# Seven small experts: taken in the order of their token counts, with fixed capacities and one loop at the end

## Chip, core and metric

The kernel runs on one core of a Trainium2 chip. The metric is the device time of one execution in microseconds, as the median of the runs shown. TensorE (PE) multiplies matrices, VectorE (DVE), ScalarE (ACT) and GpSimd (POOL) work on elements, SyncE (SP) issues most of the transfers, and POOL issues the transfers whose rows are picked by a list (gathers and scatters).

## What is computed

An attention over blocks gives x (2304 tokens, 512 wide). A dense two-layer network follows, and then a layer of eight experts, of which each token uses one, or none. Only this last layer is touched:

```python
do_compute = (x @ w_skip) > 0
xc = x[do_compute]
e_idx = np.argmax(xc @ w_gate, axis=1)
for e in range(8):
    mask = e_idx == e
    h = np.maximum(xc[mask] @ w1[e], 0.0)       # w1[e]: 512 x 1024
    y[mask] = gate_w[mask, None] * (h @ w2[e])  # w2[e]: 1024 x 512
out[do_compute] = xc + y
```

How many tokens an expert gets is known only while the kernel runs.

## The kernel before

Attention and the dense network fill the first 660 us of the profiled execution. While the dense network ends, the router writes for each token one row (place, output row, gate) into a list in DRAM, ordered by expert (`lists_d`, three copies that are summed after loading). `base` holds how far each expert's part of the list is filled, so `base - eoff` is the count of each expert.

Expert 0 has tiles of 128 tokens that are computed with split numbers, in three products for each one (`expert_tile`, L948). The first two tiles always run; `more` (L1099) runs a further one behind a condition on the count, and a loop after the fourth.

Experts 1 to 7 are computed in fp32, in the order of their numbers. Their tokens stand in groups of 32 (`MG`), because TensorE can work on four blocks of 32 columns of the stationary operand side by side: a matmul of form 128\*32 uses a quarter of the array, one of form 128\*64 a half, one of 128\*128 the whole. `Groups` (L1166) has the first product of the first group in `first`, those of the further groups in `first_rest` (L1181, each behind a condition), the turning of the hidden values in `turn` (L1149; its second half behind the condition in L1188), the second product in `second` (L1158, conditions in L1193), and the sum of the four quarters, the scaling and the scatter in `end` (L1204, L1162, L1163). `spill` (L1221) has a block of 64 tokens behind a condition (L1224) and a loop behind another (L1226). Expert 7 stands behind a condition as a whole (L1245, L1250). Each such condition is a branch on all engines, on a count that each has in a register (L1071).

`load_expert` (L838) loads the 4 MB of one expert's weights into one of four places, in eight transfers on SP's queue (L851 for w1, L853 for w2). Experts 1 and 2 are loaded ahead of the lists, 3 and 4 behind `more`, each later one behind the expert whose place it takes. For every token list, `load_lists` and `find` (L629, L624) load and sum the copies and turn them to row numbers on DVE; `gather` (L634) fetches the token rows, `turn_x` (L903) turns them on PE.

The kernel's text is written as steps; a scheduler sets the order in which small instructions stand on each engine, unless they are pinned.

Of the kernel before, what the change touches and what calls it, by code (L numbers as in the profile page):

```python
# [10 lines left out]
F32 = mybir.dt.float32  # L11
F32R = mybir.dt.float32r
BF16 = mybir.dt.bfloat16
I32 = mybir.dt.int32
# [332 lines left out]
def attention_moe_kernel(  # L347
# [716 lines left out]
    cnti = RC.tile([128, E], I32, name="cnti")  # L1064
    nc.vector.tensor_tensor(out=cnti, in0=base, in1=eoff, op=ALU.subtract)


    lall = [lists(f"la{k_}", E) for k_ in range(KS)]
    llate = lists("lx", 1)
# [13 lines left out]
    xgs.insert(4, xgf[1])  # L1083
    xts = [[M3.tile([128, ND, 128], F32R, name=f"xt{i}{j}", bufs=1) for j in range(2)] for i in range(2)]
    xts = [xtf[0], xts[0], xtf[1], xts[1]]
    fourth = lane(lall[3], 0, xgs[0], xts[2])
    xws = [CV.tile([128, ND, 128], F32, name=nm, bufs=3) for nm in ("cv2", "cv2", "cv3")]
    firsts = [lane32(lall[0], e, xgs[e % 4], xws[e % 2]) for e in range(E)]
    for lx in (firsts[1], fourth, firsts[2], firsts[3]):
        gather(lx)  # L1090

    ahead1 = [lambda: turn_x(firsts[1])]

    def later(k_):
        if k_ == 3:
            return fourth
        return lane(lall[k_] if k_ < KS else llate, 0, xgs[4 + (k_ + 1) % 2], xts[2 + (k_ + 1) % 2])

    def more(k_, lx):  # L1099
        with nullcontext() if k_ == 1 else tc.If(nreg[0] > 128 * k_):  # L1100
            if k_ < KS:
                ahead = []
                nx = later(k_ + 1)
                if k_ + 1 < KS:
                    if nx is not fourth:
                        gather(nx)
                    ahead = [lambda: turn_x(nx)]
                finish = expert_tile(lx, ahead + (ahead1 if k_ == 1 else []))
                finish()
                more(k_ + 1, nx)  # L1110
            else:
                with tc.For_i(KS, (nreg[0] + 127) // 128, 1) as i:
                    load_lists(llate, lambda l: l[bass.ds(i * 128, 128), :].unsqueeze(1), nc.sync)
                    find(llate)
                    gather(lx)
                    turn_x(lx)
                    expert_tile(lx)()

    more(1, second)
    gather(firsts[4])  # L1120
    load_expert(3)
    load_expert(4)


    MG, MH = 32, 64
    pin = tc.keep_in_program_order
    h2 = [CV.tile([128, 512], F32, name=nm, bufs=3) for nm in ("cv2", "cv3")]
    hT, ev01, ev23 = (CV.tile([128, 2, 512], F32, name="raw", bufs=3) for _ in range(3))
    ev = [ev01[:, 0], ev01[:, 1], ev23[:, 0], ev23[:, 1]]
    hx = M3.tile([128, 512], F32, name="hs")  # L1130
    for t in (*h2, hT, ev01, ev23, hx, xws[2]):
        nc.gpsimd.memset(t, 0.0)
    sums = {m: M3.tile([128, m], F32, name=f"sum{m}", bufs=1) for m in (MG, MH)}
    for m, t in sums.items():
        nc.vector.reduce_sum(out=t, in_=ident.rearrange("p (s t) -> p t s", t=m), axis=AX.X)
    bank = lambda nm: ps3.tile([128, 512], F32, name=nm, tag="ps")

    def first_product(ph, e, x, m):

        s = 128 // m  # L1140
        w = F2 // s
        for c in range(ND):
            for j in range(s):
                pin(nc.tensor.matmul(ph[j * m : j * m + m], x[:, c], weights[e][0][c][:, j * w : j * w + w], start=(c == 0), stop=(c == ND - 1)))
# [152 lines left out]
```

## Time and profile before

| | us |
|---|---|
| median of 3 runs (837.49 to 839.02) | 838.4 |
| the profiled execution, its own time | 842.87 |
| its span, first to last instruction | 841.0 |

The span is what the trace covers; 1.87 us of the profiled execution lie around it. This execution is 4.5 us longer than the median, so a difference worked out on the trace is taken from the median. All times of rows are microseconds from the span's start.

### The profile page before, as it was taken

To read this page: it belongs to the slowest core of one execution; us is meant where nothing else is said; L and a number is where in the kernel's file an instruction comes from. 1 tells how busy PE (TensorE), PEld (TensorE's weight loads), DVE (VectorE), ACT (ScalarE), POOL (GpSimd) and SP (SyncE) were. 2 spreads that over 40 slices of the span, in tenths; PEclk is the share of its full clock that TensorE was granted. 3 is DMA by queue.
4 is the path that set the end of the run, shared out by engine and by line. 5 is a ranking of instruction groups with operands and counts; after the bars stand their busy time and mean duration, and the time that the engine had idled before them with its cause. 6 is when DMAs were issued, how large, how long until landed. Compare 5 with 4: busy or idle time off the path is not lost. (4 is left out here: it accounts for less than half of the span.)

```text
span 841.0 us, 13930 instructions
## 1 busy us (share of the span) xinstructions
PE 771.7 (92%) x4662; PEld 637.6 (76%) x4662; DVE 518.4 (62%) x1134; ACT 400.9 (48%) x921; POOL 355.6 (42%) x433
## 2 busy tenths in 40 slices
PE   6788989999999989999999999999999989988883
PEld 4567878888888978898999898888898767642430
DVE  6877789886987875675663599969213632111221
ACT  6787788786977975555452222222223412111110
POOL 2755446363454664454452432562424533100211
PEclk9889999999999999999999999999999999999999
DMA  6664474454433031752233564114014944294761
GB/s 165 155 164 130 117 174 109 105 156 124 111 96 85 16 115 46 244 181 100 74 87 116 153 182 154 39 43 162 22 76 151 342 78 92 95 390 181 259 235 36
DMA packets 114546, 112.71 MB, mean 134 GB/s; under 512 B 76670, under 2 KB 79742, under 8 KB 114450
## 3 DMA queue, kind: packets, MB, share of 16 engines
q1 hardware_dynamic: 106386, 95.72, 37.9%
q0 software_dynamic: 8064, 15.80, 6.3%
q8 instruction: 49, 0.80, 0.4%
q14 instruction: 47, 0.39, 0.2%
HBM read 80.97 MB, written 22.57 MB: 123 GB/s over the span
## 5 line engine op out<-in xcount | busy, mean ns | idle before, releaser
L447 PE MATMUL ph<-xT,wbt 128*128 128x384 f32 x864 | 167.1, 338 | 3.0 <-DVE u L438 2.3
L447 PEld LDWEIGHTS ph<-xT,wbt 128*128 128x128 f32 x864 | 152.0, 188 | 12.6 <-DVE u L438 4.3
L439 POOL TENSOR_TENSOR gl<-u,gh 128x384 fp32r<-128x384 f32 x72 | 80.7, 1121 | 142.9 <-ACT gh L438 134.8
L447 PE MATMUL acc<-wbt,gh 128*128 128x512 f32 x432 | 132.9, 396 | 0.0
L185 POOL TENSOR_SCALAR P<-P,stat 128x128 f32<-128x128 f32 (+2 forms) x144 | 79.1, 570 | 76.9 <-DVE stat L183 54.7
L438 ACT CAST gh<-u 128x384 fp32r<-128x384 f32 x72 | 36.9, 513 | 119.9 <-DVE u L438 51.6
L447 PEld LDWEIGHTS acc<-wbt,gh 128*128 128x128 f32 x432 | 79.7, 188 | 12.2
L438 DVE TENSOR_TENSOR u<-ph,u 128x384 f32<-128x384 f32 x72 | 39.7, 551 | 73.1 <-ACT u L437 73.1
L447 PE MATMUL acc<-wbt,gl 128*128 128x512 f32 x216 | 81.9, 395 | 0.0
L285 PE MATMUL pv<-ph,vs 128*128 128x320 f32 (+4 forms) x280 | 71.8, 328 | 1.8 <-DVE ph L239 1.6
L236 PE MATMUL pt<-ident,P 128*128 128x128 f32 x400 | 63.6, 287 | 5.9 <-ACT P L174 2.5
L161 PE MATMUL sp<-wbt 128*128 128x128 f32 (+2 forms) x192 | 58.5, 383 | 10.6 <-DMA wbt<-wbt 3.4
L437 ACT ACTIVATE u<-ph 128x384 f32<-128x384 f32 x72 | 35.2, 488 | 64.7 <-PE ph L447 62.2
L418 POOL TENSOR_TENSOR cv<-cv,cv 128x512 int32<-128x512 int32 x32 | 42.5, 1330 | 38.7 <-DVE cv L417 33.0
L285 PEld LDWEIGHTS pv<-ph,vs 128*128 128x128 f32 x280 | 52.1, 196 | 8.4 <-DVE ph L239 2.5
L447 PE MATMUL ph<-xT,wia 128*128 128x384 f32 x288 | 56.4, 341 | 1.3 <-DVE cv L438 1.3
L236 PEld LDWEIGHTS pt<-ident,P 128*128 128x128 f32 x400 | 48.0, 146 | 11.8 <-ACT P L174 3.0
L447 PE MATMUL po<-woa,gA 128*128 128x512 f32 x216 | 55.4, 404 | 0.1
L666 DVE CUSTOM_DVE_ANT_0 xlast<-x,raw 128x512 f32<-128x512 f32 x72 | 55.0, 803 | 0.0
L243 DVE TENSOR_TENSOR pl<-pt,ph 128x512 fp32r<-128x512 f32 (+2 forms) x84 | 51.0, 624 | 5.2 <-ACT ph L242 4.2
L447 PEld LDWEIGHTS ph<-xT,wia 128*128 128x128 f32 x288 | 49.4, 188 | 2.1 <-DVE cv L438 1.6
L447 PEld LDWEIGHTS acc<-wbt,gl 128*128 128x128 f32 x216 | 40.5, 188 | 9.2
(258 smaller groups left out, 1495.8 us busy)
## 6 DMA issues: line engine op xcount, KB each, us to landing
wbt<-in_moe_w_dram SPq DMA_DIRECT2D x48, 512.0 KB, 6.5
wbt<-wbt SPq DMA_DIRECT2D x60, 144.0 KB, 2.5
raw<-in_moe_w_in_dram SPq DMA_DIRECT2D x16, 512.0 KB, 4.6
raw<-in_moe_w_out_dram SPq DMA_DIRECT2D x16, 512.0 KB, 3.6
xTd<-xT POOLq DMA_DIRECT2D x4, 1152.0 KB, 9.5
part_d<-cv SPq DMA_DIRECT2D x18, 256.0 KB, 2.1
x<-part_d SPq DMA_DIRECT2D x6, 768.0 KB, 5.2
xT<-xTd POOLq DMA_DIRECT2D x6, 768.0 KB, 6.9
```

The costliest lines, as they stand in the source:

```text
L161: nc.tensor.matmul(o_, st()[a][h][:, rows : rows + m], st()[b][:, h, c : c + w], start=(i == 0), stop=(i == 1))
L185: nc.gpsimd.tensor_scalar(out=P, in0=P, scalar1=rs[:, i : i + 1], scalar2=1.0, op0=ALU.mult, op1=ALU.mult)
L236: nc.tensor.transpose(o, src, self.ident)
L243: nc.vector.tensor_tensor(out=dl, in0=s_, in1=dh.bitcast(F32), op=ALU.subtract)
L285: nc.tensor.matmul(box["pv"][:, c0:N], v, box[t][:, i, h, cs], start=(jc == 0 and t == "ph"), stop=(jc == runs[-1][0] and t == parts[-1]))
L418: nc.gpsimd.tensor_tensor(out=w, in0=w, in1=low, op=ALU.add)
L437: nc.scalar.activation(out=u, in_=ph, func=AF.Copy, scale=0.01)
L438: return [nc.vector.tensor_tensor(out=u, in0=ph, in1=u, op=ALU.max), nc.scalar.copy(gh, u), nc.gpsimd.tensor_tensor(out=gl, in0=u, in1=gh. ...
L439: nc.gpsimd.tensor_tensor(out=gl, in0=u, in1=gh.bitcast(F32), op=ALU.subtract)]
L447: nc.tensor.matmul(ps, x, y, start=first and m == 0, stop=last and m == 3 * n - 1)
L666: nc.vector.tensor_tensor_reduce(out=junk, in0=x2[:, t], in1=wrow[j], scale=1.0, scalar=0.0, op0=ALU.mult, op1=ALU.add, accum_out=box["L"] ...
```

## The change

Experts 1 to 7 are no longer taken by number. A chain of small DVE operations ranks them by count, and makes a table `tab` with the expert's number for each rank, and rows and trips for the end. SP alone loads the seven numbers into registers, and `load_rank` (L1129 of the changed kernel) reads the weights of the expert at a rank from an address made with such a register. The places have fixed sizes, `CAPS`: rank 0 holds 192 tokens, ranks 1 to 3 hold 96 each, ranks 4 and 5 hold 32 each, rank 6 none; expert 0 has always four tiles. Rank 0 is a `Full` unit of 128 tokens, untiled (128\*128), and a `Half` unit of 64. All conditions are gone; what does not fit is done at the end by a loop over ranks and blocks of 64, behind one condition on `flag`.

```diff
-    _, nreg = nc.values_load_multi_w_load_instructions(cnti[0:1, 0:E], min_val=0, max_val=NT)
+    CAPS = (192, 96, 96, 96, 32, 32, 0, 4 * 128)
...
+    nc.vector.tensor_tensor(out=two[:, 1], in0=base[:, 1:E], in1=eoff[:, 1:E], op=ALU.subtract)
+    nc.vector.scalar_tensor_tensor(out=key, in0=two[:, 1], scalar=8.0, in1=rev[:, 1:E], op0=ALU.mult, op1=ALU.add)
+    nc.vector.tensor_tensor(out=tmp[:, :, 0], in0=key.unsqueeze(1).to_broadcast(sq), in1=key.unsqueeze(2).to_broadcast(sq), op=ALU.is_le)
+    nc.vector.reduce_sum(out=pos, in_=tmp[:, :, 0], axis=AX.X)
+    nc.vector.tensor_tensor(out=oh, in0=pos.unsqueeze(1).to_broadcast(sq), in1=rev[:, 1:E].unsqueeze(2).to_broadcast(sq), op=ALU.is_equal)
...
+    _, rank = nc.values_load_multi_w_load_instructions(tab[0:1, 0:NR, 0], engines=[mybir.EngineType.SP], min_val=1, max_val=NR)
     with tc.issue_after(end.ins):
-        for k_ in (2, 1, 0, 3):
-            load_lists(lall[k_], lambda l: l.rearrange("(e n) c -> n e c", e=E)[k_ * 128 : (k_ + 1) * 128], nc.sync)
-            find(lall[k_])
-    for e in (1, 2):
-        load_expert(e)
+        for k_ in range(2):
+            load_lists(lz[k_], lambda l: l[(2 + k_) * 128 : (3 + k_) * 128].unsqueeze(1), nc.sync)
+            find(lz[k_])
+        for k_ in range(2):
+            for t in range(TB):
+                nc.sync.dma_start(la[k_]["l3"][:, t], lists_d[t].rearrange("(e n) c -> n e c", e=E)[k_ * 128 : (k_ + 1) * 128, 1:E])
...
+    def load_rank(r, e=None, to=None):
...
+        e = rank[r] if e is None else e
+        for c in range(ND):
+            nc.sync.dma_start(a[:, c], w1[bass.ds(e, 1), c * 128 : (c + 1) * 128].rearrange("o p w -> p (o w)"))
+        for c in range(ND):
+            nc.sync.dma_start(b[:, c], w2[bass.ds(e, 1), c * 256 : (c + 1) * 256].rearrange("o (k p) w -> p (o k) w", p=128))
+    held = {r: load_rank(r) for r in range(2)}
...
+    class Full(Unit):
+        def part(self, k_):
+            ph = bank("ph3")
+            for c in range(ND):
+                pin(nc.tensor.matmul(ph, self.lx["xw"][:, c], self.w[0][c][:, k_ * 512 : k_ * 512 + 512], start=(c == 0), stop=(c == ND - 1)))
+            relu(halves[k_], ph)
...
+    units = [Full(0, 0, 0, 128), Half(1, 0, NR, MH)] + [Groups(r + 1, r, r, CAPS[r]) for r in range(1, 6)]
+    expert_tile(second, [lambda: turn_x(third)])()
+    expert_tile(third, [lambda: turn_x(fourth), units[0].turn_x])()
+    units[1].turn_x()
+    expert_tile(fourth)()
+    units[3].gather()
+    for r in (2, 3):
+        held[r] = load_rank(r)
...
+    for i, me in enumerate(units):
+        nx = units[i + 1] if i + 1 < U else None
+        if nx:
+            nx.first()
+        me.turn()
+        if nx:
+            nx.rest()
+        if i:
+            units[i - 1].end()
+            if i + 3 < U:
+                units[i + 3].gather()
+        if i + 2 < U:
+            units[i + 2].turn_x()
+        me.second()
+        if i > 0 and me.r + 4 < 6:
+            held[me.r + 4] = load_rank(me.r + 4)
...
+    with tc.If(spill > 0):
+        with tc.For_i(0, E, 1) as r:
```

The order of instructions moves at three places. On SP, before the change, two experts' weights stand ahead of the last token rows' store (`x_d<-x`), and all lists (`la2l` to `la3l`) behind it:

```order
L853 DMA wbt_7460<-in_moe_w_dram 128x2x512 x4
L851 DMA wbt_7469<-in_moe_w_dram 128x1024 x4
L853 DMA wbt_7470<-in_moe_w_dram 128x2x512 x2
L655 DMA x_d<-x_6624 128x512 x3
L658 DMA out_dram<-x_6624 128x3x512
L853 DMA wbt_7470<-in_moe_w_dram 128x2x512 x2
L1071 TENSOR_LOAD cnti
L1071 ISA x16
L631 DMA la2l_7353<-list_4115 128x8x4
```

After it, all of SP's weight transfers stand behind the load of the ranks (`tab`) and behind the last list, `la1l`:

```order
L1119 DMA la0l_7351<-list_4116 128x7x4
L1119 DMA la0l_7351<-list_4117 128x7x4
L1111 TENSOR_LOAD tab
L1111 ISA x14
L1119 DMA la1l_7354<-list_4115 128x7x4
L1119 DMA la1l_7354<-list_4116 128x7x4
L1119 DMA la1l_7354<-list_4117 128x7x4
L1142 ISA
L1142 DMA wbt_7497<-in_moe_w_dram 128x1024
```

So the weights of the first two places moved behind two waits on DVE's results. On DVE, between two steps of expert 0's second tile (`hl` is the low part of its hidden values, which PE multiplies next), two lists stood before:

```order
L632 TENSOR_REDUCE la0li<-la0l_7347 128x32
L626 TENSOR_TENSOR la0ix<-la0li,outs 128x16
L967 TENSOR_TENSOR hl<-pt,hh 128x512
L632 TENSOR_REDUCE la3li<-la3l_7356 128x32
L626 TENSOR_TENSOR la3ix<-la3li,outs 128x16
L967 TENSOR_TENSOR hl<-pt,hh 128x512
```

Now DVE ends the ranking there (`trips`, `tab`), sorts the rows of a list by rank (`rankli`), and waits for `la1l` ahead of the second `hl`:

```order
L1108 TENSOR_SCALAR trips<-trips 128x8
L1109 TENSOR_SCALAR tab<-trips 128x8
L1120 TENSOR_REDUCE la0li<-la0l_7351 128x28
L1124 TENSOR_TENSOR cv_7359<-oh_7368,la0li 128x196
L1126 TENSOR_REDUCE rankli<-cv_7359 128x28
L626 TENSOR_TENSOR rankix<-rankli,outs 128x14
L967 TENSOR_TENSOR hl<-pt,hh 128x512
L1120 TENSOR_REDUCE la1li<-la1l_7354 128x28
L1124 TENSOR_TENSOR cv_7359<-oh_7368,la1li 128x28
L1126 TENSOR_REDUCE rankli<-cv_7359 128x4
L626 TENSOR_TENSOR rankix<-rankli,outs 128x2
L967 TENSOR_TENSOR hl<-pt,hh 128x512
```

What moved is that the list on which the second `hl` now has to wait is issued by SP only behind the ranks. On PE, within one of the small experts, the groups before the change stand between branches:

```order
L1204 MATMUL py<-raw,sum_7910 32x512 x4
L1181 COMPARE_AND_BRANCH
L1144 MATMUL ph_8297<-wbt_7877,cv_7496 32x256 x16
L1181 UNCONDITIONAL_BRANCH x2
L1181 COMPARE_AND_BRANCH
L1144 MATMUL ph_8316<-wbt_7877,cv_7496 32x256 x16
L1181 UNCONDITIONAL_BRANCH x2
L1181 COMPARE_AND_BRANCH
L1144 MATMUL ph_8335<-wbt_7877,cv_7496 32x256 x16
L1181 UNCONDITIONAL_BRANCH x2
L907 MATMUL pt<-ident,xgf_4169 128x128 x4
```

After it, a unit of 96 tokens stands as one straight piece:

```order
L1177 MATMUL ph_8092<-xT_7810,cv_7534 32x256 x16
L1182 MATMUL pt<-ident,cv_7820 128x128 x4
L1182 MATMUL pt<-ident,cv_7821 128x128 x2
L1177 MATMUL ph_8120<-xT_7810,cv_7534 32x256 x16
L1177 MATMUL ph_8138<-xT_7810,cv_7534 32x256 x16
L1301 MATMUL py<-raw,sum_7826 32x512 x3
L1167 MATMUL pt<-ident,xg_7526 128x32 x4
L1191 MATMUL pp<-wbt_7801,raw 32x512 x24
```

No branch is left between the groups, the second product has three groups where a condition and a fourth stood, and the sum has three matmuls. An fp32 matmul of these lists is two instructions in the trace.

## Rows read from the trace of the kernel before

**Rows 1.** Windows: busy time by engine, then PE clock, DMA share, GB/s.

```profile
704.00:729.43 25.43, 25.43 (x120) 20.13 (x118) 5.57 (x9) 5.33 (x9) 3.01 (x3) 1.00 0.09 33
729.43:833.00 103.57, 82.58 (x874) 35.03 (x874) 19.02 (x30) 14.64 (x34) 16.31 (x17) 0.98 0.67 239
833.00:841.00 8.00, 0.00 (x0) 0.00 (x0) 0.75 (x1) 0.00 (x0) 1.00 (x1) 0.75 0.06 13
```

**Rows 2.** Groups of instructions, PE, 729.4 to 833: busy, mean ns, idle before.

```profile
L1144 PE MATMUL ph<-wbt,cv 128*32 128x256 f32 (+1 forms) x400 | 26.7, 389 | 7.0 <-ACTq L1224 2.5 <-DVEq L1224 1.9 <-PEq L1181 1.0
L1158 PE MATMUL pp<-wbt,raw 128*32 128x512 f32 (+1 forms) x208 | 26.3, 595 | 3.9 <-PEq L1250 2.1 <-PEq L1193 1.0 <-DVE raw L1150 0.8
```

**Rows 3.** Timeline, PE, the small experts: start, length, instructions, idle before.

```profile
737.58 5.39 PE L1144 MATMUL ph<-wbt,cv 128*32 128x256 f32 x96
...
758.24 7.07 PE L1158 MATMUL pp<-wbt,raw 128*32 128x512 f32 x64
...
766.42 3.65 PE L1144 MATMUL ph<-wbt,cv 128*64 128x512 f32 x16 [0.52 <-ACT cv L909]
...
772.29 3.65 PE L1158 MATMUL pp<-wbt,raw 128*64 128x512 f32 x16 [0.78 <-DVE raw L1150]
...
782.35 1.10 PE L1149 MATMUL pt<-ident,cv 128*128 128x128 f32 x8
783.38 1.06 PE L1204 MATMUL py<-raw,sum 128*32 128x512 f32 x8
784.26 3.64 PE L1144 MATMUL ph<-xT,cv 128*32 128x256 f32 x64
...
804.12 0.63 PE L907 MATMUL pt<-ident,xg 128*128 128x128 f32 x4 [0.82 <-DMA xg<-x_d,la0ix]
...
828.78 1.92 PE L1158 MATMUL pp<-wbt,raw 128*32 128x512 f32 x16 [2.12 <-PEq L1250]
831.92 1.07 PE L1204 MATMUL py<-raw,sum 128*32 128x512 f32 x8 [1.22 <-PEq L1193]
```

**Rows 4.** Untiled fp32 in attention: the forms at L285, and their timeline.

```profile
L285 PE MATMUL pv<-ph,vs x23: 219/432/537, 89.7 to 98.4; 128*128 128x320 f32 x12, 128*128 128x192 f32 x4, 128*128 128x64 f32 x4, 128*128 128x128 f32 x2
```

**Rows 5.** Timeline, PE, one stretch of these matmuls.

```profile
94.10 4.54 PE L285 MATMUL pv<-ph,vs 128*128 128x320 f32 x20 [0.83 <-DVE ph L239]
```

**Rows 6.** Timeline, PE, expert 0's second tile.

```profile
696.50 0.50 PE L919 MATMUL py<-xT,hl 128*128 128x512 f32 x1 [1.80 <-DVE hl L967]
```

**Rows 7.** Timeline, DVE, the counts, the lists and the second tile.

```profile
681.67 0.16 DVE L1065 TENSOR_TENSOR cnti<-base,eoff 128x8 int32<-128x8 f32 x1
...
689.96 0.59 DVE L1135 TENSOR_REDUCE sum<-ident 128x32 f32<-128x128 f32 x2 [2.07 <-DMA la0l<-list]
...
695.37 0.27 DVE L632 TENSOR_REDUCE la0li<-la0l 128x32 f32<-128x96 f32 x1 [1.37 <-DMA la0l<-list]
...
698.89 0.68 DVE L967 TENSOR_TENSOR hl<-pt,hh 128x512 fp32r<-128x512 f32 x1
```

**Rows 8.** Timeline, SP's queue: start and length of issuing.

```profile
668.59 1.86 SPq L853 DMA_DIRECT2D wbt<-in_moe_w_dram  x2
685.63 0.37 SPq L631 DMA_DIRECT2D la2l<-list  x1
...
691.67 1.20 SPq L631 DMA_DIRECT2D la0l<-list  x2
...
729.59 2.18 SPq L851 DMA_DIRECT2D wbt<-in_moe_w_dram  x4
...
734.41 5.70 SPq L851 DMA_DIRECT2D xT<-in_moe_w_dram  x4
```

**Rows 9.** Windows of 4 us: PE busy, PE clock, DMA share, GB/s.

```profile
697.00:701.00 4.00, 4.00 (x14) 0.57 0.67 168
...
749.00:753.00 4.00, 2.40 (x35) 1.00 1.04 390
```

**Rows 10.** Timeline, POOL, the last instruction.

```profile
834.08 1.00 POOL L1163 DMA_INDIRECT out_dram<-yo,la0ix  x1 [4.76 <-DVEq L1245]
```

More of the change, by code (lines that the diff above doesn't have):

```diff
@@ new lines, in attention_moe_kernel @@
+    caps = RC.tile([128, 2, E], F32, name="caps")
+    for r in range(E):
+        nc.gpsimd.memset(caps[:, 0, r : r + 1], float(CAPS[r]))
+        nc.gpsimd.memset(caps[:, 1, r : r + 1], float(CAPS[r] // MH * MH))
+    tab = RC.tile([128, E, 3], I32, name="tab")
+    nc.vector.tensor_copy(tab[:, :, 0], sorted_[:, 0])
+    over = sm_("over", E)
+    nc.vector.tensor_tensor(out=over, in0=sorted_[:, 1], in1=caps[:, 0], op=ALU.subtract)
+    nc.vector.tensor_scalar_max(over, over, 0.0)
+    row0 = sm_("row0", E)
@@ L1089, in attention_moe_kernel @@
[L1089 to L1125, printed above, removed]
-    pin = tc.keep_in_program_order
[L1127 to L1133, printed above, removed]
@@ new lines, in attention_moe_kernel @@
+    units = [Full(0, 0, 0, 128), Half(1, 0, NR, MH)] + [Groups(r + 1, r, r, CAPS[r]) for r in range(1, 6)]
+    U = len(units)
+    gather(third)
+    gather(fourth)
+    for i in range(3):
+        units[i].gather()
+    expert_tile(second, [lambda: turn_x(third)])()
[5 more added lines that the diff above has]
+        held[r] = load_rank(r)
+    h2 = [CV.tile([128, 512], F32, name="cv3", bufs=3) for _ in range(2)]
@@ new lines, in attention_moe_kernel @@
+    hT, ev01, ev23 = (CV.tile([128, 2, 512], F32, name="raw", bufs=3) for _ in range(3))
+    ev = [ev01[:, 0], ev01[:, 1], ev23[:, 0], ev23[:, 1]]
+    hx = CV.tile([128, 512], F32, name="cv2", bufs=3)
+    sums = {m: M3.tile([128, m], F32, name=f"sum{m}", bufs=1) for m in (MG, MH)}
+    for m, t in sums.items():
+        nc.vector.reduce_sum(out=t, in_=ident.rearrange("p (s t) -> p t s", t=m), axis=AX.X)
+    units[0].first()
+    units[0].rest()
+    for i, me in enumerate(units):
[14 more added lines that the diff above has]
+            held[me.r + 4] = load_rank(me.r + 4)
@@ new lines, in attention_moe_kernel, with half @@
+    units[-1].end()
+    flag = RC.tile([128, 1], I32, name="flag")
+    most = sm_("most", 1)
+    nc.vector.reduce_max(out=most, in_=over, axis=AX.X)
+    nc.vector.tensor_copy(flag, most)
+    _, (spill,) = nc.values_load_multi_w_load_instructions(flag[0:1, 0:1], min_val=0, max_val=NT)
+    llate = lists("lx", 1)
+    part = {k_: t[0:MH] for k_, t in llate.items()}
+    lx = lane32(llate, 0, xgs[4], xws[2])
+    to = held[3]
+    w = split(to)
+    def half(row):
+        load_lists(part, lambda l: l[bass.ds(row, MH), :].unsqueeze(1), nc.sync)
+        find(part)
+        gather_n(lx, MH)
+        turn_n(lx, MH)
```

235 lines of the change are left out of this document (141 added, 94 removed).

## The prediction

> **What bounds the kernel now.** I read the windows first, by stage [rows 1]. Up to 729.43 us PE is the bound: in expert 0's tiles it is busy all 25.43 us of the window. In the stage of experts 1 to 7 it is busy for 82.58 of 103.57 us, so 21.0 us stand idle, and 8.0 us follow behind the last matmul. DMA's mean share there is 0.67, so transfers don't fill the stage as a whole.
>
> The groups of instructions tell what PE waits for [rows 2]: the first and second products alone have 7.0 and 3.9 us of idle time, and most of their releasers end in q (ACTq, DVEq, PEq): sequencers that stand at a condition, not data. I went through PE's timeline of the stage and added up its 21 idle times (the last is the 1.22 us at 831.92): 17.5 us are released by a sequencer or by nothing that the profile shows, 3.4 us by data. The longest single one is 2.12 us, at the condition that would begin expert 7 [rows 3].
>
> The same timeline gives the counts. Expert 2 has a piece of 32 first-product instructions and one of 96 (four groups) and the block of 64 columns [rows 3]; experts 3, 4 and 5 have 32 and then 64, as at 784.26 (three groups); experts 1 and 6 have one group; expert 7 has none; expert 0 has four tiles and no loop. Sorted, this needs at most 192, 96, 96, 96, 32, 32 and 0 places and 512 for expert 0. That is `CAPS`, so the loop at the end should not run.
>
> **The stage, term by term.** I build its PE time anew from rows.
>
> A group of 32 tokens: 96 instructions of the first product take 5.39 us for three groups, 1.80 each; 64 of the second take 7.07 us for four, 1.77 each [rows 3]. Eleven groups remain (three ranks with three, two with one; before there were fifteen): 11 x 3.57 = 39.3 us.
>
> The half block: 3.65 + 3.65 = 7.3 us, as before [rows 3].
>
> The full unit does not exist in this stage before. Bounds: the 128\*64 form does 16 instructions in 3.65 us [rows 3]; if that form gained nothing from running two side by side, 16 untiled ones would take 3.65 us too, otherwise 7.3. Attention has untiled fp32 itself: 20 instructions over 12 x 320 + 4 x 192 + 4 x 64 = 4864 columns [rows 4] take 4.54 us [rows 5], 0.93 ns a column, or 7.6 us for 16 x 512 columns. I take 7.4 for each product, 14.8 us; the low end of 7.3 for both is far from the row of the same form, and I keep it for the range's foot only as a remote case. So the full unit is no cheaper than the four groups that it replaces (4 x 3.57 = 14.3 us).
>
> Sums: 8 instructions in 1.06 us [rows 3]; 24 are left (2 for the half, 2 for each group), 3.2 us. Transposes: 8 in 1.10 us [rows 3], 0.15 each; 34 of hidden values and 20 of tokens, 8.0 us. Work in all: 39.3 + 7.3 + 14.8 + 3.2 + 8.0 = 72.6 us.
>
> Waits that straight code leaves: at the end there is no next unit to put between, so the last two sums wait for ACT's copy, 1.22 us each by the row at 831.92 (it names PE's sequencer, but a copy and its landing lie in it), and the last second product for DVE's copy, 0.78 us by the row at 772.29; one gathered tile may land late, 0.82 us by the row at 804.12 [rows 3]. That makes 4.0 us, and with 1 us for transitions I call the stage 77.6 us: 26.0 less than 103.57. A count from above agrees roughly: 17.5 us of branch waits go, and of the work, sums (48 + 2 to 24 instructions, 3.4 us) and transposes (72 to 54, 2.7 us): 23.6 us. Bounds of this term: 22 to 30 us.
>
> **Weights.** They are taken away from before the lists (the last issue was at 668.59 to 670.45) and put behind the register load and the lists [rows 8]. What covers them: DVE finishes the ranking by about 694.3. This is an estimate: the chain is stuck behind the reduction at 689.96 (a pool's memory must come free, which stays so), ends that at 690.6, and has some 20 small operations to go, at 0.16 us [rows 7] to 0.25 with the wait from one to the next. The register load costs at least nothing and at most 685.63 - 681.83 = 3.8 us, the time from the counts' end on DVE to SP's first list [rows 7, 8]; a list's store lies in that too, so I take half. Three lists follow, at 0.6 us each (1.20 us for two), and weights start at about 698. At 390 GB/s [rows 9] one expert (4.2 MB) takes 10.8 us, so rank 0 is there by 709 and rank 1 by 720. They are wanted at 731 and 750: hidden, with 22 us to spare; uncovered, each us later would cost one. Ranks 2 and 3 go to places that expert 0 frees at 723 and 730 (no branch holds SP any more; before, it issued at 729.59), and are wanted 30 and 43 us into the stage (761 and 774) by the units' times above. Ranks 4 and 5 follow their places' release by 13 us or more ahead of need. Six experts are loaded instead of seven; the transfers weren't the bound, so this gains nothing.
>
> **DVE and SP around the second tile.** The first `hl` comes behind the ranking and `la0`, about when it did before (behind `la0` at 695.37), and PE's wait of 1.80 us stays. The second `hl` was at 698.89; now it waits for `la1`, which SP issues behind the register load: landing some 3 us after the last issue (`la0` too: issued by 692.87, used at 695.37), thus between 699.6 and 702.4, and `hl` 0.8 us later. PE needs it at about 701.4, 14 matmuls into this product. The wait is 0 to 2 us. [...] I take 1.5 us, bounds 0 and 3.7. Queued behind `la1` on DVE are only this tile's own steps; on SP the weights, covered as above.
>
> **Small ones.** Eight token transposes stand ahead of the stage where four stood: +0.6 us. The ranking's POOL memsets stand among work that PE does not wait for: 0. At the tail, DVE's and POOL's last steps and the store's landing stay (8.0 us); a register load on each engine and one jump over the loop come behind the last store's issue, next to its landing. POOL's issue ends at 835.08, 5.9 us before the end [rows 10], so most of the load is covered: +0.7 us, bounds 0 and 2.1, the latter by the longest jump of the stage [rows 3].
> [...]
>
> **Sum.** -26.0 + 1.5 + 0.6 + 0.7 = -23.2 us. The span goes from 841.0 to 817.8 and this execution from 842.87 to 819.7; the median, 4.5 us lower, from 838.4 to **815.2**.
>
> **Rivals.** (1) Slower: transfers with an address from a register are slow to issue. No row has one, since all stand in loops that are not entered; static ones take 0.55 us each, 1.4 where the queue is full [rows 8], and a POOL scatter takes 1.0 [rows 10]. There are 48; the last must be issued by about 802, 104 us after 698. Up to 2.2 us each they hide; from about 2.7 us each the kernel is slower than before; at 4 us the weights end at 890 and the kernel at about 905. Against it: the nearest rows are all under the limit. 4%.
> (2) The weights come late without that, because lists, gathers and weights share the engines: at half of 390 GB/s, rank 0 ends at 719.5 and rank 1 at 741, still in time, but rank 2 at 762.5 and rank 3 at 784, 1.5 and 10 us late: 817 to 825. 10%.
> (3) The pause at the second `hl` is long and the clock drops again: the 3.7 us bound, 817.5; with the tail's bound, 819. 20%, within the range.
> (4) The change does not do what it says: counts miss the capacities and the loop runs, with weights loaded again and barriers between trips: at least 15 us a trip (10.8 us of weights, then some 5 us of chain), so 831 or more. The timeline's groups say that all fits. 2%.
> (5) Straight code saves more: no wait but the last sums, and a faster full unit, 30 us less in the stage: 808 to 811. 20%.
> My forecast has the rest, 44%.
>
> **Numbers.** Likeliest 815.2 us; the range 808 to 822 takes in (3), (5) and most of (2). 0.2% is 1.7 us, about what a measurement can tell here. Faster by more than that: all but (1) and what is unforeseen, 0.94; within it 0.02; slower 0.04.
>
> **What would show it.** In the changed profile: the stage from the first full-unit matmul to the last sum is about 78 us, and no idle time of PE there is released by a sequencer; the full unit's products take 7.4 us each; the first weights are issued near 698, 0.6 us apiece, and no PE matmul waits for a DMA into `wbt` or `xT`; `la1li` on DVE stands ahead of a late second `hl`; the tail is 8 to 10 us. The prediction is wrong if PE waits for weights, or if the stage keeps idle times of 10 us or more from another releaser.

## The result and the profile after

The changed kernel takes **809.37 us** (median of 4 runs, 807.44 to 810.45) against 838.71 us before (4 runs on the same chip): ratio 0.9647, 95% interval 0.9622 to 0.9671, so 29.3 us less. The prediction was 815.2 us with a range of 808 to 822; the time lies in the range, 5.8 us from its likeliest value and inside the 808 to 811 us of the rival "straight code saves more", to which the prediction gave 20%.

The profiled execution took 807.44 us, span 805.7. I cut it in three as [rows 1]: the front, from the end of PE's wait for `xtf` in expert 0's first tile (665.76 us before, 660.05 after) to the first matmul of the small experts; their stage; the tail behind the last matmul. Before, these are 63.67, 103.57 and 8.0 us. Windows of the changed kernel (length, PE busy, then the other engines, PE clock, DMA share, GB/s):

```profile
660.05:723.06 63.01, 57.99 (x293) 45.98 (x294) 25.32 (x85) 13.76 (x25) 14.82 (x14) 0.97 0.70 231
723.06:797.30 74.24, 73.06 (x671) 30.68 (x669) 14.53 (x26) 12.58 (x28) 10.32 (x11) 1.00 0.59 217
797.30:805.70 8.40, 0.00 (x1) 0.00 (x0) 0.74 (x1) 0.00 (x0) 0.87 (x1) 0.59 0.04 10
```

The whole gain stands in the stage: 29.3 us shorter, and PE now busy for 73.06 of its 74.24 us. PE's groups in the stage, which answer to [rows 2] (busy us, mean ns, idle before and its releaser):

```profile
L1191 PE MATMUL pp<-wbt,raw 128*32 128x512 f32 (+1 forms) x144 | 19.7, 595 | 0.0
L1177 PE MATMUL ph<-wbt,cv 128*32 128x256 f32 (+1 forms) x272 | 19.3, 394 | 0.0
L1239 PE MATMUL py<-wbt,raw 128*128 128x512 f32 x16 | 7.1, 594 | 0.0
L1223 PE MATMUL ph<-wbt,cv 128*128 128x512 f32 x16 | 7.0, 592 | 0.0
L1301 PE MATMUL py<-raw,sum 128*32 128x512 f32 x22 | 5.2, 594 | 1.2 <-ACT raw L1296 1.2
```

The products had 10.9 us of idle time ahead of them before, most of it released by sequencers; they have none now, and no row waits for a transfer. The full unit is L1223 and L1239, 7.0 and 7.1 us. PE's timeline has two idle times in the stage, at its end, and one ahead of it, in expert 0's second tile (start, length, instructions, idle before):

```profile
693.26 0.80 PE L919 MATMUL py<-xT,hl 128*128 128x512 f32 x1 [2.26 <-DVE hl L967]
...
758.52 1.07 PE L1264 MATMUL py<-raw,sum 128*64 128x512 f32 x2
...
771.30 1.03 PE L1301 MATMUL py<-raw,sum 128*32 128x512 f32 x6
...
792.72 0.62 PE L1301 MATMUL py<-raw,sum 128*32 128x512 f32 x1 [0.40 <-ACT raw L1296]
...
796.26 1.04 PE L1301 MATMUL py<-raw,sum 128*32 128x512 f32 x2 [0.78 <-ACT raw L1296]
```

The rows at 758.52 and 771.30 are sums without a wait; a later section needs them. The idle time of 2.26 us took the place of the 1.80 us of [rows 6]. DVE's and SP's timelines show whose it is, and answer to [rows 7, 8]:

```profile
685.09 0.17 DVE L1109 TENSOR_SCALAR tab<-trips 128x8 int32<-128x8 int32 x1
685.19 0.26 DVE L1120 TENSOR_REDUCE la0li<-la0l 128x28 f32<-128x84 f32 x1
...
691.70 0.25 DVE L1120 TENSOR_REDUCE la1li<-la1l 128x28 f32<-128x84 f32 x1 [4.25 <-DMA la1l<-list]
...
692.52 0.69 DVE L967 TENSOR_TENSOR hl<-pt,hh 128x512 fp32r<-128x512 f32 x1
```

```profile
686.90 1.59 SPq L1119 DMA_DIRECT2D la1l<-list  x3
688.75 3.12 SPq L1142 DMA_DIRECT2D wbt<-in_moe_w_dram  x4
...
723.36 1.96 SPq L1142 DMA_DIRECT2D xT<-in_moe_w_dram  x4
```

SP can load the seven numbers once `tab` is done at 685.26; its next issue, of the list `la1l`, comes at 686.90, 1.64 us later. The list lands by 691.70, DVE stands 4.25 us for it with the second `hl` queued behind, and PE stands 2.26 us for that `hl`. Transfers whose address comes from a register are issued in 0.49 us each where SP waits for no earlier transfer (four in 1.96 us at 723.36; the next four take 5.09 us at 725.51, with 3.0 us of such waits), as quickly as the static 0.55 of [rows 8].

### The profile page after: what moved, and what is told of

It is laid out like the page before. It is cut to its first block, busy times and chain, and to the rows that moved or that the text cites. A ratio compares the mean times of both kernels' runs of the same rounds, so it can differ in the third digit from the quotient of the medians.

```text
span 805.7 us, 13115 instructions
## 1 busy us (share of the span) xinstructions
PE 753.8 (94%) x4462; PEld 627.9 (78%) x4463; DVE 515.1 (64%) x1159; ACT 398.6 (49%) x917; POOL 344.7 (43%) x437
## 3 DMA queue, kind: packets, MB, share of 16 engines
q0 software_dynamic: 7264, 13.50, 5.7%
## 4 chain that ended last, share of the span: by engine, by line
PE 60%; DVE 21%; ACT 9%; issue 4%; DMA 3%; POOL 1%; SPq 1%; POOLq 0%; ACTq 0%; DVEq 0%
PE ph L447 15%; PE acc L447 12%; DVE xlast L666 9%; PE po L447 5%; PE pv L285 4%; PE sp L161 3%; PE ph L1177 3%; PE pt L236 3%; PE pp L1191 3%; PE py L919 2%; DMA wbt<-wbt 2%; PE ph L919 1%; ACT P L177 1%; ACT ph L242 1%; PE big L100 1%
## 5 line engine op out<-in xcount | busy, mean ns | idle before, releaser
L285 PE MATMUL pv<-ph,vs 128*128 128x320 f32 (+4 forms) x280 | 69.1, 317 | 1.8 <-DVE ph L239 1.6
L161 PE MATMUL sp<-wbt 128*128 128x128 f32 (+2 forms) x192 | 56.8, 374 | 12.2 <-DMA wbt<-wbt 3.3
L285 PEld LDWEIGHTS pv<-ph,vs 128*128 128x128 f32 x280 | 50.4, 189 | 7.5 <-DVE ph L239 2.3
L447 PEld LDWEIGHTS po<-woa,gA 128*128 128x128 f32 x216 | 40.9, 193 | 8.6 <-DVE tm L299 0.2
```

What stands on the lines that cost most here:

```text
L161: nc.tensor.matmul(o_, st()[a][h][:, rows : rows + m], st()[b][:, h, c : c + w], start=(i == 0), stop=(i == 1))
L285: nc.tensor.matmul(box["pv"][:, c0:N], v, box[t][:, i, h, cs], start=(jc == 0 and t == "ph"), stop=(jc == runs[-1][0] and t == parts[-1]))
L447: nc.tensor.matmul(ps, x, y, start=first and m == 0, stop=last and m == 3 * n - 1)
```

## The experiments

**What was to be told apart.** My theory: the gain is the conditions. Its main rival: fixed, sorted places gain by packing and by one load less, and waits for data would stand where the conditions' waits are taken out. In the table the front, the stage and the tail are those of each kernel's profiled execution; ratios are to the kernel before, run on the same chip, with 95% intervals. In run 12 the stage's first matmuls stand among expert 0's last ones, so its front and stage are given as one.

| kernel | median us | ratio | front | stage | tail |
|---|---|---|---|---|---|
| before | 838.71 | 1 | 63.67 | 103.57 | 8.0 |
| changed | 809.37 | 0.9647 (0.9622 to 0.9671) | 63.01 | 74.24 | 8.40 |
| 1 before, no branches | 816.72 | 0.9738 (0.9691 to 0.9784) | 61.53 | 82.32 | 7.54 |
| 2 changed, entered conditions | 818.12 | 0.9769 (0.972 to 0.9818) | 70.35 | 76.81 | 7.81 |
| 3 changed, skipped blocks of 64 | 815.78 | 0.9732 (0.9688 to 0.9776) | 68.52 | 76.24 | 7.15 |
| 4 changed, four groups for full | 809.36 | 0.9665 (0.9612 to 0.9718) | 64.14 | 75.67 | 8.38 |
| 5 before, no conditions of spill | 834.49 | 0.9947 (0.9922 to 0.9972) | 63.93 | 96.48 | 10.22 |
| 6 before, no conditions of groups | 824.45 | 0.9816 (0.9788 to 0.9845) | 61.33 | 90.07 | 8.03 |
| 7 changed, skipped groups | 828.99 | 0.9887 (0.9849 to 0.9925) | 68.66 | 86.58 | 7.74 |
| 8 changed, skipped nested blocks | 822.47 | 0.9808 (0.9786 to 0.983) | 68.81 | 79.59 | 6.90 |
| 9 changed, lists before the load | **805.32** | 0.9593 (0.9567 to 0.9618) | 61.41 | 74.24 | 8.41 |
| 10 changed, no loop at the end | 809.12 | 0.9645 (0.9614 to 0.9675) | 65.04 | 74.24 | 6.86 |
| 11 changed, fixed weight numbers | 808.90 | 0.964 (0.9609 to 0.9671) | 64.71 | 74.25 | 8.40 |
| 12 as 9, flag loaded early | 806.65 | 0.9623 (0.9588 to 0.9658) | with stage: 134.59 | | 8.37 |

### 1. The kernel before without its branches

```diff
-            with tc.If(self.n > g * MG):
+            if CNT[self.e] > g * MG:
...
-        with tc.If(nreg[e] > 128):
+        if CNT[e] > 128:
...
```

Expert 0's conditions and the load of the counts into registers go too.

> The kernel before, its conditions resolved when it is written, from this input's counts (466, 26, 180, 67, 72, 79, 26, 0): no branch is left, nothing else moves (same expert order, same fifteen groups of 32, same early static weight loads, expert 7's load too). It leaves out any other counts, and the steps of expert 7, which has no token. My theory (the gain is mostly the waits of sequencers at conditions, 17.5 us of PE's idle time in the stage before): 17 to 20 us less than the kernel before, 819 to 822 us, with PE idle for under 5 us in the stage; the other 9 to 12 us of the change are then fewer sums, transposes, the full unit, and waits. Rival P (the fixed places, sorted, do it by packing and by loading six experts in place of seven; the branches' waits only stand beside waits for data, which appear when they go): 0 to 8 us less, 831 to 839 us, with the idle time now released by DVE, ACT or DMA.

2.6% less, some 20 us by the medians, as the theory has it: two thirds of the gain come with no sorting, no capacities, no register address and seven loads. Windows and two of PE's groups in the stage of this kernel:

```profile
726.64:808.96 82.32, 77.71 (x875) 33.67 (x874) 19.00 (x30) 15.38 (x34) 14.76 (x15) 1.00 0.73 267
```

```profile
L1146 PE MATMUL ph<-wbt,cv 128*32 128x256 f32 (+1 forms) x400 | 26.0, 389 | 1.6 <-issue 1.1 <-ACT cv L909 0.5
L1160 PE MATMUL pp<-wbt,raw 128*32 128x512 f32 (+1 forms) x208 | 25.5, 594 | 0.8 <-DVE raw L1152 0.8
```

Idle time falls from 21.0 to 4.6 us, none of it released by a sequencer, so few waits for data appear (3.4 us stood there before). But the stage is 21.25 us shorter, and only 16.4 of that is idle time: PE's busy time falls too, from 82.58 to 77.71 us, with 874 instructions before and 875 here. The conditions' price is partly inside rows that count as busy. The single instruction takes no longer: the mean of these two groups is 389 and 595 ns before [rows 2], 389 and 594 here. The instructions of a group overlap (400 of 389 ns stand in 26.7 us of busy time before, in 26.0 here), and with the conditions they overlap less, which the profile counts as busy time. Another part is the clock. The kernel before has two windows in its stage with

```profile
777.43:781.43 4.00, 2.91 (x29) 1.71 (x32) 0.74 (x1) 0.00 (x0) 1.46 (x2) 0.69 0.61 195
781.43:785.43 4.00, 4.00 (x52) 2.00 (x48) 1.39 (x2) 0.39 (x1) 0.46 (x1) 0.88 1.03 403
```

a granted clock of 0.69 and 0.88, behind idle times of 0.74 and 1.09 us; 32 matmuls that take 1.9 us elsewhere take 3.57 there (row at 778.85 of its timeline). Here the stage has 1.00.

### 2 and 3. Conditions put back into the changed kernel

Run 2 puts conditions that are true around groups (and clears a few tiles on POOL); run 3 a block that is never entered behind each of six units, without the loop at the end.

```diff
+    _, nreg = nc.values_load_multi_w_load_instructions(cntr[0:1, 0:NR], min_val=0, max_val=NT)
...
-                self.product(g)
-                self.relu(g)
+                with tc.If(nreg[self.r] > g * MG):
+                    self.product(g)
+                    self.relu(g)
...
```

> The changed kernel with thirteen conditions put back around the second and later groups of each unit (first product, second turning, second product); all are true for this input, so every block is entered and no work changes. The counts are loaded in registers on all engines behind the ranking. Theory A (each condition costs, entered or not): 13 times 0.8 to 1.3 us, 10 to 17 us more than the changed kernel, 819 to 826 us. [...]

```diff
+    _, nreg = nc.values_load_multi_w_load_instructions(cntr[0:1, 0:NR], min_val=0, max_val=NT)
...
         me.second()
+        if i:
+            with tc.If(nreg[me.r] > CAPS[me.r]):
+                half(me)
```

> The changed kernel with a block of 64 tokens (all engines take part) behind a condition after the second product of each of the units 1 to 6; the condition is false for this input each time, so six blocks are jumped over. The loop at the end is taken out. It leaves out counts over the capacities beyond the 64 tokens of each block. Theory B (a block jumped over costs PE 1 to 2 us, as the 2.12 us at expert 7's condition): 6 to 12 us more than the changed kernel, 815 to 821 us, with PE idle that much more in the stage and released by sequencers. [...]

By the totals (8.7 and 6.4 us more than the changed kernel, medians taken at different times) theory B would look right in run 3, and theory A nearly so in run 2. The traces say otherwise: the stage is only 2.57 and 2.00 us longer, and the rest is in the front. PE's timeline in run 2, and two of its windows:

```profile
687.32 6.78 PE L919 MATMUL ph<-wbt,xtf 128*128 128x512 f32 x19 [5.31 <-DVE trips L1108]
```

```profile
686.00:690.00 4.00, 2.68 (x6) 2.17 (x7) 2.15 (x14) 0.00 (x0) 2.35 (x3) 0.50 0.54 84
690.00:694.00 4.00, 4.00 (x15) 3.17 (x14) 0.00 (x0) 0.60 (x1) 1.47 (x2) 0.75 0.60 175
```

and the same in run 3:

```profile
688.68 7.25 PE L919 MATMUL ph<-wbt,xtf 128*128 128x512 f32 x19 [5.40 <-DVE trips L1107]
```

Loading the counts into PE's registers behind the ranking makes PE stand for the ranking, 5.3 us in the middle of a tile where the changed kernel waits 1.56 us for a turned tile, and then run at 0.50 of its clock. The kernel before loads its counts as well, but behind `cnti` at 681.67 [rows 7], and its PE shows no such wait. So it is the place of the load in these experiments, where neither kernel has one on PE, that makes most of both totals. In the stage, fifteen entered conditions (the expectation's thirteen is a miscount) cost 2.57 / 15 = 0.17 us each, six skipped plain blocks 0.33 us each. Theory A falls at its price of 0.8 to 1.3 us a condition, theory B in run 3 at its price of 1 to 2 us a block. So a new question: why do the conditions of the kernel before cost 21 us?

### 4. Four groups in place of the full unit

```diff
-    units = [Full(0, 0, 0, 128), Half(1, 0, NR, MH)] + ...
+    units = [Groups(0, 0, 0, 128), Half(1, 0, NR, MH)] + ...
```

> The changed kernel with rank 0's unit of 128 tokens as four groups of 32, as the kernel before did it; everything else stays. My theory (the full unit works at the rate of the groups, 6.96 + 6.99 us against 4 x 3.57 = 14.3): 0.3 us more of products, four or six more sums at 0.15 us and two waits more, together 0.5 to 1.5 us more than the changed kernel, 810 to 811 us. Rival (the full unit is a large part of the gain beyond the branches): 4 us more or above, 813 us.

The stage is 1.43 us longer (75.67), the median the same within its interval. The longer part is work: PE is busy for 74.39 us against 73.06, and its two last waits are the same (0.40 and 0.78 us). Eight sums more take about 1.0 us, and the two products of the unit 14.4 us against 14.0, read from the start of one row to the start of the next. So the untiled form saves sums and has hardly a rate of its own.

### 5 and 6. Which conditions of the kernel before

Run 5 resolves those of the 64-column blocks, run 6 those of the groups.

```diff
-        with tc.If(nreg[e] > 128):
+        if CNT[e] > 128:
             half(e, lx)
-            with tc.If(nreg[e] > 128 + MH):
-                ...
```

> The kernel before, with the conditions of the 64-column blocks alone (two nested ones and a loop per expert) resolved from this input's counts; the conditions of the groups, of expert 0's tiles and of expert 7 stay. It leaves out counts other than this input's over 128. All conditions together cost 20 us. Theory N (a jump over a long block with a nested condition and a loop is what costs; the waits put down to ACT's and DVE's sequencers at these blocks, 0.73 + 1.09 + 1.76 + 1.85 + 1.65 = 7.1 us, and the low clock behind two of them): 12 to 16 us less than the kernel before. Theory K (the short blocks of the groups cost as much each, and there are more of them): 4 to 7 us less. Theory C (the conditions' costs overlap, each hides part of another): under 4 us less here and under 8 in the next kernel.

```diff
-                with tc.If(self.n > g * MG):
+                if CNT[self.e] > g * MG:
...
-            with tc.If(self.n > 2 * MG):
+            if CNT[self.e] > 2 * MG:
```

> The kernel before, with the conditions of the groups alone resolved (first product, second turning, second product of experts 1 to 7); the nested blocks of 64 columns, expert 0's tiles and expert 7's condition stay. It leaves out other counts up to 128. Theory N: 3 to 7 us less than the kernel before. Theory K: 11 to 15 us less. Theory C: under 8 us less.

0.5% and 1.8% less, 4.4 and 15.4 us by the ratios (the second just above its 11 to 15): theory K, the short blocks of the groups carry most. In the stage the two take 7.09 and 13.50 us, together 20.6 of the 21.25 that run 1 took, so the prices add up and hardly overlap, though run 1 also resolves the conditions of experts 0 and 7. The windows of the stages, of run 5 and then of run 6:

```profile
729.00:825.48 96.48, 82.05 (x875) 35.85 (x874) 18.73 (x30) 14.82 (x34) 16.24 (x17) 1.00 0.69 253
```

```profile
724.70:814.77 90.07, 79.46 (x874) 33.53 (x874) 18.91 (x30) 15.28 (x34) 16.28 (x17) 1.00 0.76 274
```

Run 5 gives 2.2 us of its gain back in the tail (10.22 us). There POOL's last scatter stands for the landing of the one before it and starts 2.94 us behind the last matmul's end; before, it starts 1.08 us behind it (834.08 in [rows 10], 833.00 in [rows 1]):

```profile
828.42 0.98 POOL L1163 DMA_INDIRECT out_dram<-yo,la0ix  x1 [3.20 <-DMA out_dram<-yo,la0ix]
```

### 7 and 8. The same kinds of block in the changed kernel

```diff
-            for g in range(1, self.n // MG):
-                self.product(g)
-                self.relu(g)
+            for g in range(1, 4):
+                with tc.If(nreg[self.r] > g * MG) if g >= self.n // MG else nullcontext():
+                    self.product(g)
+                    self.relu(g)
...
```

> The changed kernel with the groups beyond each capacity put back behind conditions (20 blocks: first product, turning, second product; none is entered here), counts loaded in registers on all engines behind the ranking. The load of the counts alone cost PE a wait of 5.3 us and its lower clock in the runs with entered conditions and with skipped blocks of 64, so the total is 5 to 8 us up for it; the stage itself (74.24 us in the changed kernel) decides. Theory K: 8 us or more longer, 82 us or above. Theory N: 1 to 3 us longer. Theory C: 1 to 4 us longer.

Run 8's edit is shown against run 3, which it starts from:

```diff
             with tc.If(nreg[me.r] > CAPS[me.r]):
-                half(me)
+                half(me, CAPS[me.r])
+                with tc.If(nreg[me.r] > CAPS[me.r] + MH):
+                    with tc.For_i(1, (nreg[me.r] - CAPS[me.r] + MH - 1) // MH, 1) as j:
+                        half(me, j * MH + CAPS[me.r])
```

> The changed kernel with six skipped blocks of 64 tokens as in the run with skipped blocks, but each with a second condition and a loop inside, as the kernel before has them. The loop at the end is out, and the counts are loaded in registers (5 to 8 us as there). The stage was 76.24 us with six plain blocks. Theory N: 4 us or more longer than that, 80 us or above, PE idle 1 to 1.8 us at each block. Theories K and C: 76 to 78 us.

Twenty skipped short blocks make the stage 12.34 us longer, 0.62 us each: theory K again. Window and timeline of run 7's stage:

```profile
731.98:818.56 86.58, 79.90 (x671) 33.29 (x669) 14.63 (x26) 12.54 (x28) 10.32 (x11) 1.00 0.52 189
```

```profile
775.08 1.49 PE L1194 MATMUL pp<-wbt,raw 128*32 128x512 f32 x11 [0.15 <-PEq L1301]
...
796.31 0.40 PE L1170 MATMUL pt<-ident,xg 32*128 32x32 f32 x4 [1.21 <-PEq L1288]
...
806.91 0.42 PE L1180 MATMUL ph<-wbt,cv 128*32 128x256 f32 x3 [1.52 <-PEq L1288]
```

A single skip in a unit of three groups shows at most 0.15 us of idle time, three in a row in a unit of one group 1.0 to 1.5 us. And again a half of the price isn't idle time: the same 671 instructions, at a clock of 1.00, are busy for 79.90 us against 73.06. The largest group, in run 7 and then in the changed kernel, has the same mean and more busy time; its rows stand further apart:

```profile
L1180 PE MATMUL ph<-wbt,cv 128*32 128x256 f32 x256 | 18.9, 382 | 1.8 <-PEq L1288 1.7
```

```profile
L1177 PE MATMUL ph<-wbt,cv 128*32 128x256 f32 x256 | 15.4, 381 | 0.0
```

Six nested blocks cost 79.59 - 74.24 = 5.35 us, 0.89 each, against 0.33 for plain ones. That lies between the two expectations: nesting does cost, but only the first idle time (1.88 us) reaches the size of theory N. Here 4.65 of the 5.35 us are idle time (PE is busy for 73.76 us). Two idle times of run 8:

```profile
762.86 1.93 PE L1180 MATMUL ph<-wbt,cv 128*32 128x256 f32 x32 [1.88 <-ACTq L1367]
...
790.34 1.07 PE L1180 MATMUL ph<-wbt,cv 128*32 128x256 f32 x16 [0.81 <-ACTq L1367]
```

With these prices the kernel before can be counted. By its token counts its stage skips 20 group blocks (seven each for the experts with 26 tokens, two each for those with 67, 72 and 79), enters 22 and passes six nested blocks: 20 x 0.62 + 22 x 0.17 + 6 x 0.89 = 21.5 us, against the 21.25 that run 1 measured. That the sum is so close is partly luck. The split fits less well (16.1 for the groups, 13.5 measured; 5.3 for the nested ones, 7.1 measured), one of the six nested blocks is entered (expert 2's, up to its second condition), and the conditions of experts 0 and 7, 0.65 and 2.12 us of idle time in this stage, aren't in the count.

### 9 to 12. The front, the weights and the tail

```diff
-    _, rank = nc.values_load_multi_w_load_instructions(tab[0:1, 0:NR, 0], engines=[mybir.EngineType.SP], ...)
     with tc.issue_after(end.ins):
...
+    with tc.issue_after(la1_last.ins):
+        _, rank = nc.values_load_multi_w_load_instructions(tab[0:1, 0:NR, 0], engines=[mybir.EngineType.SP], ...)
```

> The changed kernel with SP's register load of the sorted experts' numbers put behind the lists of la1, and so in front of the weights alone. My theory (the second wait for hl, 2.26 us, is that list, late by the load's time on SP): la1li follows la0li on DVE at once, the 2.26 us go and up to 1 us of low clock behind them; weights start when they did; 2 to 3.5 us less than the changed kernel, 806 to 807.5 us. Rival (PE meets the next late thing there, hl or xt of the same tile, or the first hl's wait comes back): 0 to 1 us less, 808.5 to 809.5 us.

This is 4.0 us less than the changed kernel by the medians, and the intervals of the two ratios don't meet (those of runs 10 and 11, taken beside it, just touch its own). By its median it is the fastest version that was run, and it computes everything. Its front, PE's and DVE's rows, and SP's:

```profile
664.54:725.95 61.41, 57.79 (x293) 46.04 (x294) 25.40 (x85) 13.77 (x25) 14.84 (x14) 0.97 0.69 226
```

```profile
694.32 0.50 PE L919 MATMUL py<-xT,hl 128*128 128x512 f32 x1 [0.99 <-DVE hl L967]
```

```profile
692.76 0.25 DVE L1119 TENSOR_REDUCE la1li<-la1l 128x28 f32<-128x84 f32 x1 [0.43 <-DMA la1l<-list]
```

```profile
688.88 1.78 SPq L1118 DMA_DIRECT2D la1l<-list  x3
694.97 2.20 SPq L1144 DMA_DIRECT2D wbt<-in_moe_w_dram  x4
```

The wait of 2.26 us at the second `hl` is gone; one of 0.99 us at the first stands there. Profiles of the front differ in one more thing, a dip of the clock 8 to 12 us into it. The kernel before and runs 9, 10 and 11 have it; the changed kernel and runs 4 and 12 don't: nine matmuls of L919, 6.4 us into the front, take 3.37 us before and 3.07, 3.12 and 3.26 in runs 9, 10 and 11, but 2.33, 2.34 and 2.34 in the other three. Here are the kernel before, run 10 and the changed kernel:

```profile
673.76:677.76 4.00, 4.00 (x23) 2.77 (x21) 2.49 (x17) 1.11 (x3) 0.00 (x0) 0.65 0.39 147
```

```profile
672.86:676.86 4.00, 4.00 (x22) 2.76 (x20) 1.96 (x9) 0.89 (x2) 0.00 (x0) 0.61 0.00 0
```

```profile
672.05:676.05 4.00, 3.44 (x20) 2.90 (x18) 1.52 (x8) 0.58 (x1) 0.97 (x1) 1.00 0.01 4
```

So like goes with like. With this dip, run 9's front is 3.3 to 3.6 us shorter than those of runs 11 and 10, which have the list behind the register load as the changed kernel has it. Without it, run 12's front (60.35 us, if its stage is run 9's 74.24) is 2.7 shorter than the changed kernel's. That is within the 2 to 3.5 us expected, or just above. By the medians the size is less sure: run 12 contains the same change, and its interval overlaps that of the changed kernel. Weights that start 1.7 us later, counted from the front's start, cost nothing (the stage is 74.24 us again).

```diff
-    with tc.If(spill > 0):
-        with tc.For_i(0, E, 1) as r:
-            ...
```

> The changed kernel without the flag, its register loads, the condition and the loop at the end. It leaves out what exceeds the capacities (nothing does here). My theory (the tail grew by 0.4 us by the traces, 8.01 to 8.40): 0.3 to 1 us less than the changed kernel, 808.4 to 809.1 us, with the tail at 7.4 to 8 us. [...]

```diff
-        e = rank[r] if e is None else e
+        e = (2, 5, 4, 3, 1, 6)[r] if e is None else e
```

> The changed kernel with the six experts' numbers fixed when it is written (2, 5, 4, 3, 1, 6), so that the weights' transfers have constant addresses, need no register load, and the first two experts' start ahead of the lists as in the kernel before. The lists are sorted as in the changed kernel. It leaves out every other order of the experts. My theory (the weights are hidden either way): the stage within 0.5 us of 74.24 us; in front of it the second hl's wait goes (no register load in front of la1), but the lists queue behind the weights' issues and the first hl's wait of 1 to 2 us comes back: in all 2 us less to 1 us more, 807.5 to 810.5 us. Rival (register addresses and late loads cost part of the gain): 4 us less or more, 805 us or below.

Both have the changed kernel's time. Run 11's stage is the same to 0.01 us, with constant addresses and two experts' weights ahead of the lists: neither the register addresses nor the late loads cost anything there. The expectation for it was wrong in one point: the register load stays in that kernel, though nothing reads it, and with it the wait at the second `hl` (2.28 us). Together with run 9 this puts that wait on the register load in front of the list, not on the weights. Run 10's tail is 6.86 us against 8.40, below the 7.4 to 8 expected: the unentered loop costs 1.5 us there. The table's other tails put it lower: 7.15 and 6.90 us in runs 3 and 8, which have no loop, 7.81 and 7.74 in runs 2 and 7, which keep it. 1.5 us lie within the intervals of the medians, which therefore can't show it.

```diff
+    _, (spill,) = nc.values_load_multi_w_load_instructions(flag[0:1, 0:1], min_val=0, max_val=NT)
     units[0].first()
...
-    _, (spill,) = nc.values_load_multi_w_load_instructions(flag[0:1, 0:1], min_val=0, max_val=NT)
```

> The kernel with the lists before the load, and the flag of the loop at the end loaded in registers ahead of the stage, while PE works on expert 0's last tile, in place of behind the last store; the condition and the loop stay at the end. By the traces the loop and its flag make the tail 8.40 us, against 6.86 without them. Theory (the load is most of these 1.5 us): the tail is 7.0 to 7.6 us and the kernel 0.8 to 1.4 us below the one with the lists before the load. Rival (the jump over the loop is most of it): the tail stays at 8.2 to 8.4 us, no gain. Rival (the load holds up PE's sequencer where it now stands): PE idle for about 1 us or more near the end of expert 0's last tile, no gain or 1 us more.

Run 12 is run 9 with this edit. The tail stays at 8.37 us, against 6.86 without the loop (run 10): what costs there is the condition and the jump, not the load of the flag. The first rival holds; the load costs PE nothing visible at its new place (between an `hl` at 689.89 us and the last sums its PE has no idle time). The kernel is not faster than run 9.

## Why the prediction was right, and where its sizes were off

**The mechanism** holds: sequencers at conditions were most of the stage's idle time (16.4 of 21.0 us go in run 1), and their removal is most of the gain (run 1: some 20 of 29 us). The time is not that of the forecast itself but of its fifth rival, which said that the stage would give 30 us. That all tokens fit, that the loop isn't entered and that the weights are hidden all came out; the slower rival (register addresses above 2.7 us each) falls with 0.49 us, and that of late weights with a stage in which no row waits for a transfer.

**The stage** was to be 77.6 us and is 74.24. The term "waits that straight code leaves" is the one that failed: 4.0 us and 1.0 for transitions, where 1.2 us were measured. The last sums wait 0.40 and 0.78 us, not twice 1.22 (there was a sequencer in that row, as the text itself said); the wait of 0.78 us for DVE's copy and that of 0.82 us for a gathered tile, both taken from rows of before, don't exist in the changed kernel. Straight code alone doesn't take the first away: run 1 still has 0.8 us for DVE's `raw` (L1160). It goes with the new order of the units.

**The work** was predicted as 72.6 us and is 73.06, and that it is so close is luck. Read from the start of one row of PE's timeline to the start of the next, the sums take about 5.9 us in place of 3.2. They were priced by the instruction, eight in 1.06 us, but two take 1.07 us and six 1.03 (758.52, 771.30): here a bundle of two costs as much as one of six or eight. Terms that were too high hide this: the full unit is 13.95 us in place of 14.8, the transposes 6.9 in place of 8.0. The groups (39.0) and the half block (7.3) were right.

**The check from above** gave 23.6 us for the stage and was too low because it counted a condition's price by idle time alone, 17.5 us. Run 1 shows 21.25: some 5 us lay in rows that the profile calls busy. What is left to sorting and packing is 82.32 - 74.24 = 8.1 us, 4.65 of PE's busy time and 3.4 of waits, against 6.1 for sums and transposes. This is a remainder: but for the full unit (run 4) no run takes it apart.

**The front** was to be 2.1 us longer. The second `hl` does wait, 2.26 us and at a lower clock behind it (0.59 in the window from 693.05 to 697.05), against 1.5 taken and 3.7 as the bound. The clock's part in these two figures was an estimate (a clock of 0.57 over 4 us, as in [rows 9], loses 1.7 us), and no run shows it by itself; the runs show the wait and the 0.59. But the first `hl`'s 1.80 us, which was said to stay, went: DVE has `la0` at 685.19, 8.98 us after POOL issues the first of the list's three stores (676.21), against 12.06 us before (683.31 to 695.37), where the loads of other lists stood ahead of it on SP. The ranking also ended earlier than estimated, 25.2 us into the front (685.26) and not 28.5 (694.3). The changed kernel's front is 0.7 us shorter, but its profile lacks the early dip of the clock; runs 11 and 10, which have it as the kernel before has, are 1.0 and 1.4 us longer. And the old order has itself a front of 61.33 us in run 6, where the first `hl` waits 0.94 us. So the forecast's direction is likely right, and its size stays open. **The tail** grew by 0.4 us where 0.7 was taken, with 2.1 as the bound, from a row of 2.12 us. The loop's whole price by run 10 is 1.5 us, between the two, and less by runs 2, 3, 7 and 8. But the tail before wasn't free of such a price either (8.0 us, and 7.54 in run 1 without any condition).

**The sum** by these windows: -29.3 in the stage, -0.7 to +1.4 in the front, +0.4 in the tail, -29.6 to -27.5 us against 29.3 by the medians. The profiled executions differ by 35.4 us; 5.7 us of it stand ahead of the front, in attention and the dense network, where the executions differ anyway: the front begins between 663.4 and 665.8 us in the four profiles of the kernel before and its variants, between 659.0 and 664.9 in the ten of the changed kernel and its variants. The change moves two experts' weight loads out of the end of that piece, where the first was issued at 633.11 us. But 5.5 of the 5.7 us stand before it: the last issue of SP ahead of it that both kernels have, a store of L658, is at 614.65 us before and 609.15 after. So at most some 0.2 us can belong to these loads.

## What to carry to other kernels

Price a data-dependent condition by its kind (entered, skipped, several in a row) and from a kernel without it, since idle time shows only a part (16.4 of 21.25 us here; the other 4.9 stood in rows of matmuls that count as busy). Read where an experiment's time went before its total confirms a theory; here one total fitted a theory and another came within 1 us of one, and their traces refute both, because a load of registers stood in PE's way. A register load held its engine's queue here until the value existed (PE stands 5.3 us in run 2; in the changed kernel SP issues nothing from 683.24 to 686.90 us), so what others wait for, like a short list, is issued ahead of it.

## What the runs showed of the hardware

- Conditions on all engines, in PE's time within this stage: 0.17 us entered, 0.33 us for a skipped plain block of 64 tokens, 0.62 for a skipped short block, 0.89 for a skipped block with a condition and a loop inside. That a short block costs more than a long one was not expected. It stands more often in a row with others and with less work ahead, but how the price divides is open. Of the 0.62 us 0.28 are idle time, of the 0.89 us 0.78.
- The instruction queues of the page moved 49 + 47 packets in the kernel before, 37 + 30 in run 1, 36 + 34 in the changed one and in run 2, 37 + 33 in run 3, 40 + 36 in run 7, 40 + 42 in run 8. Six packets more for twenty skips on five engines: their number doesn't explain the price of the skips. What a jump waits for, no run shows.
- Seven registers on SP cost 1.64 us from the value to the next issue. A register in a transfer's address cost nothing that was seen (0.49 us an issue against 0.55; a stage of 74.24 us against 74.25 with constant addresses).
- Untiled fp32 (128\*128) does 16 matmuls of 512 columns in 7.0 us, close to four column groups side by side (64 of form 128\*32 in 7.07 us [rows 3]).
